# RWKV-6 attention and an MLP on one core: round 1's r-u-k sums from natural k and r, round 2's work one slot ahead, second products in runs of three

## The chip, the cores and the metric

One Trainium2 chip, one core. The metric is the device time in microseconds (us) of one execution, inputs and output in HBM. The kernel before takes 566.72 us (median of three runs, 566.61 to 567.1). The profiled execution has a span of 564.6 us.

## The reference, cut to what matters

B = 4 batches, H = 8 heads, S = 768 steps, D = 48; x has 384 columns, the MLP 1536 hidden ones. All is float32.

```python
# attention with decay, for every batch and head
for t in range(S):
    cur = einsum(u * k[t], v[t])                 # outer product
    y[t] = einsum(r[t], state + cur)             # the u term: (sum_d r*u*k) * v[t]
    state = w[t][:, None] * state + einsum(k[t], v[t])
x = y as (B, S, H*D)
# MLP
xn = (x - mean) / sqrt(var + 1e-6) * g_ln
out = x + maximum(xn @ w_ch1, 0) @ w_ch2
```

The change concerns the u term: for every step and head the sum over d of r\*u\*k, which multiplies v. It needs r and k as they lie in HBM ("natural": step in the partition), or turned (d in the partition), with a matmul to sum over partitions.

## The kernel before

A *unit* is four heads of one batch over 384 steps, a *round* two units (all eight heads), and there are eight rounds. A round goes through six levels: at each one, `quads` (TensorE, into `a_ps`) makes the products inside blocks of growing length, and `grow` (VectorE) multiplies r and k (`rkT`) by decays, so that the next level finds them ready. Then come `ends` (transposes of k, `kn_ps`), `states` (`kv`, then the chain `s` on VectorE) and `outputs` (`y`, then `x` on VectorE). Between these, `fill` places the steps of the MLP of the round before, three matmuls each, and a list of other tasks. TensorE, ScalarE (ACT), VectorE (DVE) and GpSimd (POOL) run their instructions in the order of this text; transfers given to `SP` may be issued earlier than they stand.

```python
def own_products(q, eng):                  # r*u*k in natural form
    rk = st[q]["ruk"] = p1.tile([P, TT, NH, D], F32, tag="rk")
    eng.tensor_tensor(out=rk, in0=nat["k"][q % 2][..., 0:D], in1=nat["r"][q % 2][..., 0:D], op=ALU.mult)
    eng.tensor_tensor(out=rk, in0=rk, in1=u_bc[...].broadcast_to(...), op=ALU.mult)
    if q >= FIRST * U:                     # FIRST = 3, U = 2
        k1 = nat["w"][0][..., 0:D]         # k of the step before
        eng.tensor_tensor(out=k1, in0=k1, in1=nat["r"][q % 2][..., 0:D], op=ALU.mult)

def own_sums(q):                           # VectorE: own, and next from round 3 on
    DVE.tensor_reduce(out=o, in_=st[q]["ruk"], axis=AX.X, op=ALU.add)
    ...

def products(q, eng=DVE):                  # rounds 0 and 1: r*k of the turned form
    eng.tensor_tensor(out=ruk, in0=a["r"], in1=a["k"], op=ALU.mult)

def product_sums(q):                       # 12 matmuls with u, 128x2 each: own_ps
    for pr in pairs:
        for c in range(TT):
            PE.matmul(ps[:, ts(pr * TT + c, 2)], a["ruk"][pr][:, ts(c, P)], sel[:, NP * g + pr], ...)
    ACT.copy(out=own, in_=ps)

def own_term(q, eng):                      # vo = v * own, and from round 3 on the step before's
    ...

def stage(q, nm, pr, eng=SP):              # 4 transfers into a "raw" buffer (4 of them): w_runs, k_runs, r_runs
def squares(q, nm, pr):                    # VectorE transposes from there into wT or rkT, rounds from 3 on

def mlp(rnd):
    for f in range(FC):                    # 12 steps of the first product: h_ps
        ...                                # three matmuls, then ACT relu: h
    groups = ((0, 1), (2,)) if rnd == 0 else ((0,), (1,), (2,))
    at = 0
    for group in groups:                   # second product: o_ps, one PSUM bank for each i
        for f in range(FC):
            converted(len(parts) - FC + f + 1)    # round 0: VectorE has joined so many weight parts
            for i in group:
                PE.matmul(ps[i], hs[f][:, ts(i, P)], w2_sb[:, f, :], start=f == 0, stop=f == FC - 1)
                at += 1
                if at % KC == 0 and f < FC - 1:
                    yield                  # KC = 3
        for i in group:
            DVE.tensor_tensor(out=o, in0=ps[i], in1=x[:, i], op=ALU.add)
            ...
```

h_ps and o_ps share two PSUM banks. In the MLP of round 0 the weights are still being split: ScalarE writes parts (`w_sb`, `held`, `rest`) and VectorE joins them. The loop of rounds, cut to what the change touches:

```python
for rnd in range(1, NR + 1):               # old, now, new: units of rnd-1, rnd, rnd+1
    for lev in range(NLEV):
        # states and outputs of old; quads, grow, keep of now
        ...
        if rnd == 2 and lev == 2:
            for q in now:
                take(DVE, q)               # own_products and own_sums, at once
                tasks += each(load, new[q % U :][:1], "kr")
        first = 3 if rnd == 2 else 1
        if rnd > 1 and new and first - 1 <= lev < first + 3:
            m = lev - first
            turns = [(new, "w"), (new[:1], "kr"), (new[1:], "kr")]
            if m >= 0:
                tasks += each(squares, *turns[m], pairs)
            if m < 2:
                tasks += each(stage, *turns[m + 1], pairs)
        ...
        fill(UNTIL[slot], tasks)           # MLP steps spread among the tasks
```

Of the kernel before, what the change touches and what calls it, by code (L numbers as in the profile page):

```python
# [9 lines left out]
F32 = mybir.dt.float32  # L10
# [42 lines left out]
def kernel(  # L53
# [68 lines left out]
    def load(q, which="wkr", eng=SP):  # L122
        for nm in which:
            for c in range(TT):
                eng.dma_start(
                    out=nat[nm][q % 2][:, c, :, 0:D],
                    in_=steps({"w": w, "k": k, "r": r}[nm], q, c),
                )
# [200 lines left out]
    def converted(n):  # L329
        while joined < n:  # L330
            join()
# [76 lines left out]

    def own_products(q, eng):
        b, f, g = units[q]  # L410
        rk = st[q]["ruk"] = p1.tile([P, TT, NH, D], F32, tag="rk", name=f"rk{q}")
        eng.tensor_tensor(
            out=rk, in0=nat["k"][q % 2][..., 0:D], in1=nat["r"][q % 2][..., 0:D], op=ALU.mult
        )
        eng.tensor_tensor(
            out=rk, in0=rk,
            in1=u_bc[:, ts(g, NH)][:, None].broadcast_to([P, TT, NH, D]), op=ALU.mult,
        )
        if q >= FIRST * U:
# [12 lines left out]
    def products(q, eng=DVE):  # L432
        a = st[q]

        if q < U:
            ruk = p2.tile([P, TT, H, D], F32, tag="x", name=f"ruk{q}")
            ruk = ruk.rearrange("p c h d -> p (c h d)")[:, 0:W]
        else:
            ruk = p2.tile([P, NK, P], F32, tag="kn", name=f"ruk{q}")
            ruk = ruk.rearrange("p k t -> p (k t)")  # L440
        a["ruk"] = [ruk[:, ts(pr, RN)] for pr in pairs]
        eng.tensor_tensor(out=ruk, in0=a["r"], in1=a["k"], op=ALU.mult)

# [265 lines left out]
    def mlp(rnd):  # L709
        b, f0 = rounds[rnd]  # L710
        x, xT, name = xs[b, f0], xTs[rnd], f"{b}_{f0}"
        hs = []
        for f in range(FC):
            converted(KC * (f * P // WC + 1))
            ps = ps_m.tile([P, RN], F32, tag="m", name=f"h_ps{name}_{f}")
            for kc in range(KC):
                PE.matmul(
                    ps, w1_sb[:, kc, ts(f, P)], xT[:, kc, :], start=kc == 0, stop=kc == KC - 1
                )
            hs.append(ph.tile([P, RN], F32, tag="h", name=f"h{name}_{f}"))  # L720
            ACT.activation(out=hs[f], in_=ps, func=AF.Relu)
            yield

        groups = ((0, 1), (2,)) if rnd == 0 else ((0,), (1,), (2,))
        at = 0
        for group in groups:
            ps = {
                i: ps_m.tile([P, H, D], F32, tag="m", name=f"o_ps{name}_{i}") for i in group
            }
            for f in range(FC):  # L730
                converted(len(parts) - FC + f + 1)
                for i in group:
                    PE.matmul(
                        ps[i].rearrange("p h d -> p (h d)"), hs[f][:, ts(i, P)],
                        w2_sb[:, f, :], start=f == 0, stop=f == FC - 1,
                    )
                    at += 1
                    if at % KC == 0 and f < FC - 1:
                        yield
            for i in group:  # L740
                o = p2.tile([P, H, D], F32, tag="o", name=f"o{name}_{i}")
                DVE.tensor_tensor(out=o, in0=ps[i], in1=x[:, i], op=ALU.add)
                SP.dma_start(
                    out=out[b, ds(f0 * RN + i * P, P), :].rearrange("t (h d) -> t h d", d=D),
                    in_=o,
                )
            yield
# [50 lines left out]
    FIRST = 3  # L798
    odd = const.tile([P, 1], F32, name="odd")

    def take(eng, q):

        own_products(q, eng)
        own_sums(q)


    (u0, u1), new = units_of(0), units_of(1)
    warm(8)
# [21 lines left out]
    begin()  # L830
    begin()
    load(new[1], "k", SPO)
    warm(3)
    grow(u1, 0)
    keep(0, 0)
# [22 lines left out]
    states(u0, "m")  # L858
    own_term(u0, POOL)
    finish(2)  # L860
    products(new[0], POOL)
    exchanged(u0)
    states(u1)
    product_sums(u1)
    own_term(u1, POOL)
    own_outputs(u0)
    warm(3, "t")
    outputs(u0)
# [14 lines left out]
    begin()  # L883
    join()
    join()
    products(new[1])
    run(each(turned_x, [0], range(KC)))
    mlps.append(mlp(0))

# [9 lines left out]
    for rnd in range(1, NR + 1):  # L899
# [3 lines left out]
        for lev in range(NLEV):  # L903
# [22 lines left out]
            if rnd == 1:  # L926
                if lev < 2:
                    tasks += each(load, new, "kr"[lev], [SPO])
                if lev == 2:
                    SPO.dma_start(  # L930
                        out=u_bc,
                        in_=bass.AP(
                            tensor=u.tensor, offset=u.offset, ap=[[0, P], [D, H], [1, D]]
                        ),
                    )
                    tasks += each(load_v, now, [SPO])
                if lev == 3:
                    tasks += each(load_vx, now, [SPO])
                if lev in (4, 5):
                    own_term(now[lev - 4], POOL)  # L940
# [5 lines left out]
                )  # L946
            if rnd == 2 and lev == 2:
                for q in now:
                    take(DVE, q)
                    tasks += each(load, new[q % U :][:1], "kr")  # L950
            if rnd == 2 and lev in (3, 4):
                tasks += each(own_term, now[lev - 3 :][:1], [POOL])
            if rnd > 2 and lev == 1:
                tasks += each(load, new, ["kr"])
            first = 3 if rnd == 2 else 1
            if rnd > 1 and new and first - 1 <= lev < first + 3:
                m = lev - first
                turns = [(new, "w"), (new[:1], "kr"), (new[1:], "kr")]
# [13 lines left out]
            if lev == 3 and rnd > 1:  # L972
                for q in now:
                    load_vx(q)
                for q in new:
                    load_v(q)
                if new:
                    load_before(new[0], k, 0)
                    load_before(new[0], v, 1)
                if rnd > 2:  # L980
                    moments(rnd - 1)
                    tasks = each(norm, [rnd - 1]) + tasks
            if lev == 4 and rnd > 2:
                tasks += each(turned_x, [rnd - 1], range(KC))
            if lev == 4 and rnd > 1:
                tasks += each(own_products, new[:1], [POOL])
            if lev == NLEV - 1:

                if now:
                    mlp_step()  # L990
                if rnd >= 2 and new:
                    own_sums(new[0])
                if rnd >= 2:
                    tasks += each(load_before, new[1:], [k], [0])
                    tasks += each(own_term, new[:1], [POOL])
                    tasks += each(load_before, new[1:], [v], [1])
                    tasks += each(own_products, new[1:], [POOL])
                    tasks += each(own_sums, new[1:]) + each(own_term, new[1:], [POOL])
                    if new:
                        tasks += each(totals, [rnd + 1], [POOL])  # L1000
                if now:
                    tasks = mixed(
                        tasks,
                        each(ends, now, pairs) + each(finish, [2, 2, 4])
                    )
                if rnd == 1:
                    tasks = [join] * JOINS[lev] + tasks + each(totals, [rnd + 1], [POOL])
            if rnd == 1 and lev < NLEV - 1:

                n = (1, 2, 2, 1, 0, 0)[lev] * NP  # L1010
                tasks += mixed(
                    [begin] * BEGINS[lev], [join] * JOINS[lev], ahead[:n],
                    each(product_sums, now) if lev == 1 else [],
                )
                del ahead[:n]
            fill(UNTIL[slot], tasks)
# [34 lines left out]
```

## Time and profile before

| | |
|---|---|
| time | 566.72 us |
| span of the profiled execution | 564.6 us |
| mean granted TensorE clock | 0.988 |
| DVE TENSOR_TENSOR ruk, 128x768 (3) | 951 ns each |
| POOL TENSOR_TENSOR ruk, 128x768 (1) | 1816 ns |
| POOL TENSOR_TENSOR rk, 128x576 | 1410 ns median |
| DVE TENSOR_TENSOR rk, 128x576 | 750 ns median of the first product |
| DVE TENSOR_REDUCE own, 128x576 to 128x12 | 752 ns median |
| ACT COPY own from own_ps | 170 ns |
| DVE STREAM_TRANSPOSE, four of w_runs | 2.9 us |

Durations are of single instructions, read from the groups of one tile. Engines: PE is TensorE, PEld its weight loads, DVE VectorE, ACT ScalarE, POOL GpSimd, SPq the sync engine's queue, which issues transfers. A float32 matmul of the source stands as two in the trace, so a step of three is x6. "A <- B" in a list of waits means that A waited for B. The names of lines (L49 and such) are those of a helper and tell little; tiles tell the operations apart.

### The profile page before, as it was taken

What the parts mean: (1) busy time and instruction counts of PE and PEld (TensorE: products, weight loads), DVE (VectorE), ACT (ScalarE), POOL (GpSimd) and SP (SyncE); (2) the same over time, 40 slices, a digit from 0 to 9 for tenths busy, and PEclk for the clock granted to TensorE, in tenths of its full rate; (3) what the DMA queues carried; (4) which work ended last, traced back from release to release, by engine and by line L of the source; (5) the groups of instructions that cost most, each with busy time, mean ns of one, the idle gap of its engine ahead of it and who ended that gap; (6) DMA issues with size and microseconds to landing.
All of it is one profiled execution on the core that took longest, in us unless ns stands there. A gap on an engine that the chain in (4) does not pass through costs nothing.

```text
span 564.6 us, 18202 instructions
## 1 busy us (share of the span) xinstructions
PE 548.6 (97%) x7898; PEld 359.3 (64%) x7898; DVE 332.1 (59%) x654; ACT 168.7 (30%) x363; POOL 134.8 (24%) x157
## 2 busy tenths in 40 slices
PE   9999998998889999999999999999999999999997
PEld 6777665675555666666666666666666666665554
DVE  4888998859777685757386655666472611130000
ACT  2576887502250015301421025201421025102200
POOL 6140010204194019401590029021640000000000
PEclk9899999999997999999999999999999999999999
DMA  9947887245566455646474646545200000000000
GB/s 231 195 127 144 209 215 193 57 94 100 127 153 145 123 125 119 137 102 147 95 140 99 139 106 136 119 120 118 58 1 2 31 15 1 2 29 15 0 15 28
DMA packets 141552, 56.64 MB, mean 100 GB/s; under 512 B 124448, under 2 KB 130720, under 8 KB 141472
## 3 DMA queue, kind: packets, MB, share of 16 engines
q1 hardware_dynamic: 139600, 54.88, 43.1%
q8 instruction: 62, 1.02, 0.8%
q10 hardware_dynamic: 1872, 0.59, 0.4%
q14 instruction: 18, 0.15, 0.1%
HBM read 48.66 MB, written 4.72 MB: 95 GB/s over the span
## 4 chain that ended last, share of the span: by engine, by line
PE 82%; DVE 9%; ACT 3%; DMA 2%; issue 2%; SPq 1%; POOL 0%; ACTq 0%; DVEq 0%; POOLq 0%
PE o_ps L49 33%; PE h_ps L49 27%; PE a_ps L49 9%; PE y L49 5%; DVE rkT L49 3%; DVE w_sb L49 2%; PE kv L49 2%; PE kn_ps L49 2%; DMA nat_r<-in_r_dram 1%; ACT rest L49 1%; PE xT_ps L49 1%; PE own_ps L49 1%; PE idle L49 1%; PE k_ps L49 1%; DVE A L49 1%
## 5 line engine op out<-in xcount | busy, mean ns | idle before, releaser
L49 PE MATMUL o_ps<-w_sb,h 128*128 128x384 f32 x576 | 200.2, 497 | 1.0 <-ACT h L49 1.0
L49 PE MATMUL h_ps<-xT,w_sb 128*128 128x384 f32 x576 | 196.4, 491 | 2.5 <-DVE o L49 1.4
L49 PEld LDWEIGHTS h_ps<-xT,w_sb 128*128 128x128 f32 x576 | 105.6, 190 | 70.3 <-DVE o L49 2.0
L49 PEld LDWEIGHTS o_ps<-w_sb,h 128*128 128x128 f32 x576 | 106.6, 192 | 67.8 <-issue 2.4
L49 DVE TENSOR_TENSOR rkT<-rkT,tot 128x768 f32<-128x768 f32 (+1 forms) x96 | 77.4, 849 | 27.6 <-issue 17.6
L49 ACT ACTIVATE h<-h_ps 128x384 f32<-128x384 f32 x96 | 46.9, 488 | 142.6 <-PE h_ps L49 142.4
L49 PEld LDWEIGHTS a_ps<-rkT 48*64 48x64 f32 x4128 | 65.7, 137 | 23.5 <-issue 12.5
L49 PE MATMUL a_ps<-rkT 48*64 48x32 f32 x4128 | 70.7, 221 | 3.4 <-DVE rkT L49 3.3
L49 DVE TENSOR_TENSOR o<-o_ps,x 128x384 f32<-128x384 f32 x24 | 13.3, 553 | 95.6 <-PE o_ps L49 95.5
L49 POOL TENSOR_TENSOR vo<-v,own 128x576 f32<-128x576 f32 x16 | 19.1, 1194 | 106.4 <-DVE own L49 62.5
L49 ACT ACTIVATE rstd<-mv,eps 128x3 f32<-128x3 f32 x8 | 2.4, 296 | 133.9 <-DVE mv L49 133.9
L49 DVE SCALAR_TENSOR_TENSOR s<-s,decay,kv 128x48 f32<-128x48 f32 x160 | 29.3, 256 | 18.9 <-PE kv L49 18.9
L49 POOL TENSOR_TENSOR nat_w<-nat_w,nat_r 128x576 f32<-128x576 f32 x10 | 14.4, 1436 | 103.1 <-DMA nat_w<-in_v_dram 70.5
L49 DVE COPY_PREDICATED A<-mask,a_ps 128x768 f32<-128x768 int8 x32 | 38.3, 1198 | 0.0
L49 DVE TENSOR_TENSOR x<-y,vo 128x288 f32<-128x288 f32 x32 | 13.1, 452 | 36.7 <-PE y L49 36.7
L49 ACT ACTIVATE xT<-xT_ps,g_sb 128x384 f32<-128x384 f32 x24 | 13.6, 579 | 48.4 <-PE xT_ps L49 48.4
L49 DVE TENSOR_TENSOR rkT<-rkT,wT 128x768 f32<-128x768 f32 x16 | 24.9, 1591 | 0.9 <-PE a_ps L49 0.8
L49 DVE TENSOR_REDUCE own<-rk 128x12 f32<-128x576 f32 x12 | 9.0, 749 | 23.6 <-POOL rk L49 23.5
L49 DVE TENSOR_SCALAR w_sb<-w_sb 128x384 f32<-128x384 f32 (+1 forms) x48 | 19.5, 407 | 0.8
L49 PEld LDWEIGHTS y<-v,A 64*64 64x64 f32 x384 | 13.4, 139 | 7.6 <-issue 4.4
L49 DVE STREAM_TRANSPOSE rkT<-r_runs 128x384 f32<-128x384 f32 x20 | 15.6, 840 | 3.2 <-DMA r_runs<-in_r_dram 3.2
L49 POOL TENSOR_TENSOR tot<-wT 128x768 f32<-128x768 f32 x6 | 12.4, 2072 | 20.2 <-DVE rkT L49 20.2
(88 smaller groups left out, 546.9 us busy)
## 6 DMA issues: line engine op xcount, KB each, us to landing
raw<-in_moe_w_ch_dram SPq DMA_DIRECT2D x24, 384.0 KB, 3.8
w_runs<-in_w_dram SPq DMA_DIRECT2D x79, 70.0 KB, 2.1
k_runs<-in_k_dram SPq DMA_DIRECT2D x79, 70.0 KB, 2.0
r_runs<-in_r_dram SPq DMA_DIRECT2D x79, 70.0 KB, 2.0
v<-in_v_dram SPq DMA_DIRECT2D x48, 96.0 KB, 2.9
out_dram<-o SPq DMA_DIRECT2D x24, 192.0 KB, 2.5
nat_r<-in_r_dram SPq DMA_DIRECT2D x42, 96.0 KB, 3.2
nat_k<-in_k_dram SPq DMA_DIRECT2D x42, 96.0 KB, 3.2
```

The source lines that it names most:

```text
L49: return lambda *args, **kw: self.tc.keep_in_program_order(f(*args, **kw))
```

## The change

It does four things.

- Round 1 takes its r-u-k sums from natural k and r, as later rounds do: two products on GpSimd for its first unit and on VectorE for its second, and reduces on VectorE, in place of a product of the turned form, 12 matmuls and a ScalarE copy for each unit. `u_bc`, which these products need, is loaded earlier.
- In the MLP of round 0 the second product goes in runs of three matmuls of one bank, in place of alternating between two.
- In round 2 the turning of round 3's w, k and r (stage and squares) is one slot, that is one level, earlier; the own products of round 2 become tasks.
- From round 2 on, GpSimd's chain (own products and own terms of the next round, with the transfers for it) is placed one slot earlier, and so are VectorE's sums of it.

The aim is to take work from TensorE and to have the next round's operands ready sooner.

```diff
     def own_products(q, eng):
-        rk = st[q]["ruk"] = p1.tile([P, TT, NH, D], F32, tag="rk", name=f"rk{q}")
+        if q < 2 * U:
+            rk = p2.tile([P, NK, P], F32, tag="kn", name=f"rk{q}")
+            ...
+        else:
+            rk = p1.tile([P, TT, NH, D], F32, tag="rk", name=f"rk{q}")
+        st.setdefault(q, {})["ruk"] = rk
...
-            for f in range(FC):
-                converted(len(parts) - FC + f + 1)
+            for f0_ in range(0, FC, KC):
+                converted(len(parts) - FC + f0_ + KC)
                 for i in group:
-                    PE.matmul(...hs[f]...)
-                    at += 1
-                    if at % KC == 0 and f < FC - 1:
+                    for f in range(f0_, f0_ + KC):
+                        PE.matmul(...hs[f]...)
+                    if f < FC - 1 or i != group[-1]:
                         yield
...
     load(new[1], "k", SPO)
+    SPO.dma_start(out=u_bc, ...)                 # was in round 1, level 2
...
-    products(new[0], POOL)
     exchanged(u0)
     states(u1)
     product_sums(u1)
     own_term(u1, POOL)
+    own_products(new[0], POOL)
...
-    products(new[1])
+    own_products(new[1], DVE)
...
             if rnd == 2 and lev == 2:
                 for q in now:
-                    take(DVE, q)
+                    tasks += each(own_products, [q], [DVE]) + each(own_sums, [q])
                     tasks += each(load, new[q % U :][:1], "kr")
+            if rnd >= 2 and lev == 2 and new:
+                tasks += each(load_before, new[:1], [k], [0]) + each(load_v, new[:1])
+                tasks += each(load_before, new[:1], [v], [1])
+            if rnd >= 2 and lev == 3:
+                tasks += each(load_v, new[1:])
...
-            first = 3 if rnd == 2 else 1
+            first = 2 if rnd == 2 else 1
...
             if lev == 3 and rnd > 1:
                 for q in now:
                     load_vx(q)
-                for q in new:
-                    load_v(q)
-                if new:
-                    load_before(new[0], k, 0)
-                    load_before(new[0], v, 1)
...
             if lev == 4 and rnd > 2:
                 tasks += each(turned_x, [rnd - 1], range(KC))
+                if rnd > 2 and new:
+                    tasks += each(own_sums, new[:1])
+            if lev == 3 and rnd > 1:
+                tasks += each(own_products, new[:1], [POOL])
             if lev == 4 and rnd > 1:
-                tasks += each(own_products, new[:1], [POOL])
+                if rnd == 2:
+                    tasks += each(own_sums, new[:1])
+                tasks += each(load_before, new[1:], [k], [0])
+                tasks += each(own_term, new[:1], [POOL])
+                tasks += each(load_before, new[1:], [v], [1])
+                tasks += each(own_products, new[1:], [POOL])
             if lev == NLEV - 1:
-                if rnd >= 2 and new:
-                    own_sums(new[0])
                 if rnd >= 2:
-                    tasks += each(load_before, new[1:], [k], [0])
-                    tasks += each(own_term, new[:1], [POOL])
-                    tasks += each(load_before, new[1:], [v], [1])
-                    tasks += each(own_products, new[1:], [POOL])
                     tasks += each(own_sums, new[1:]) + each(own_term, new[1:], [POOL])
...
-                    each(product_sums, now) if lev == 1 else [],
+                    each(own_sums, now) if lev == 1 else [],
```

More of the change, by code (lines that the diff above doesn't have):

```diff
@@ L410, in own_products @@
         b, f, g = units[q]
-        rk = st[q]["ruk"] = p1.tile([P, TT, NH, D], F32, tag="rk", name=f"rk{q}")
+        if q < 2 * U:
+            rk = p2.tile([P, NK, P], F32, tag="kn", name=f"rk{q}")
+            rk = rk.rearrange("p k t -> p (k t)")[:, 0 : TT * NH * D]
+            rk = rk.rearrange("p (c h d) -> p c h d", c=TT, h=NH)
+        else:
+            rk = p1.tile([P, TT, NH, D], F32, tag="rk", name=f"rk{q}")
+        st.setdefault(q, {})["ruk"] = rk
         eng.tensor_tensor(
@@ L433, in products @@
         a = st[q]
[L435 to L440, printed above, removed]
+        ruk = p2.tile([P, TT, H, D], F32, tag="x", name=f"ruk{q}")
+        ruk = ruk.rearrange("p c h d -> p (c h d)")[:, 0:W]
         a["ruk"] = [ruk[:, ts(pr, RN)] for pr in pairs]
@@ L724, in mlp @@
         groups = ((0, 1), (2,)) if rnd == 0 else ((0,), (1,), (2,))
-        at = 0
         for group in groups:
@@ L729, in mlp @@
             }
-            for f in range(FC):
-                converted(len(parts) - FC + f + 1)
+            for f0_ in range(0, FC, KC):
+                converted(len(parts) - FC + f0_ + KC)
                 for i in group:
[L733 to L736, printed above, removed]
-                    at += 1
-                    if at % KC == 0 and f < FC - 1:
+                    for f in range(f0_, f0_ + KC):
+                        PE.matmul(
+                            ps[i].rearrange("p h d -> p (h d)"), hs[f][:, ts(i, P)],
+                            w2_sb[:, f, :], start=f == 0, stop=f == FC - 1,
+                        )
+                    if f < FC - 1 or i != group[-1]:
                         yield
@@ L799 @@
     odd = const.tile([P, 1], F32, name="odd")
-    def take(eng, q):
-        own_products(q, eng)
-        own_sums(q)
     (u0, u1), new = units_of(0), units_of(1)
@@ L832 @@
     load(new[1], "k", SPO)
+    SPO.dma_start(
+        out=u_bc, in_=bass.AP(tensor=u.tensor, offset=u.offset, ap=[[0, P], [D, H], [1, D]])
+    )
     warm(3)
@@ L929 @@
                 if lev == 2:
[L930 to L935, printed above, removed]
                     tasks += each(load_v, now, [SPO])
```

## Prediction

> **What bounds the kernel now.** I read the page first: who is busy, and where the busy share dips.
>
> ```profile
> PE 548.6 (97%) x7898; PEld 359.3 (64%) x7898; DVE 332.1 (59%) x654; ACT 168.7 (30%) x363; POOL 134.8 (24%) x157
> ...
> PE   9999998998889999999999999999999999999997
> ...
> DVE  4888998859777685757386655666472611130000
> ...
> PEclk9899999999997999999999999999999999999999
> ```
>
> TensorE is busy for 97%; the dips are in slices 7 to 12, and the clock dips in slice 13. From 171 us on nothing is to be won: the windows show PE busy for all of 171.0-218.5, 218.5-281.1, 281.1-343.7 and 343.7-406.3. So the answer lies before 171 us. Next view, the windows of that part (columns: window, its length, then PE, PEld, DVE, ACT and POOL busy with counts, clock, DMA share, GB/s):
>
> ```profile
> 60.00:70.00 10.00, 9.37 (x51) 6.40 (x49) 9.35 (x19) 7.54 (x19) 0.00 (x0) 1.00 0.96 213
> ...
> 90.00:100.00 10.00, 8.95 (x121) 5.31 (x120) 8.92 (x21) 5.58 (x12) 0.42 (x1) 1.00 0.75 184
> ...
> 130.00:140.00 10.00, 8.63 (x118) 5.24 (x117) 9.83 (x10) 1.18 (x3) 5.43 (x4) 1.00 0.76 135
> 140.00:150.00 10.00, 10.00 (x214) 6.69 (x213) 8.03 (x11) 1.96 (x4) 2.85 (x2) 1.00 0.43 103
> 150.00:160.00 10.00, 8.50 (x79) 5.17 (x78) 7.69 (x12) 5.00 (x12) 4.58 (x4) 1.00 0.57 144
> 160.00:171.00 11.00, 8.16 (x126) 4.94 (x128) 8.60 (x19) 4.11 (x9) 10.21 (x8) 0.98 0.73 163
> ```
>
> Two stages have holes: 50-100 us, where VectorE is filled over 90% (it splits the MLP's weights there, beside round 1), and 120-171 us, round 2. PE's own waits in 118-172 us name the holes (who waits, for whom: us in total, times, longest), and short windows show what the last one does to the clock:
>
> ```profile
> PE a_ps L49 <- DVE rkT L49: 3.3, 3, 1.7
> PE h_ps L49 <- DVE o L49: 1.4, 1, 1.4
> PE kn_ps L49 <- DVE rkT L49: 1.2, 1, 1.2
> ```
>
> ```profile
> 168.00:170.00 2.00, 0.90 (x48) 0.82 (x48) 2.00 (x2) 0.00 (x0) 1.92 (x2) 1.00 0.70 167
> 170.00:171.00 1.00, 0.29 (x12) 0.29 (x15) 0.89 (x2) 0.00 (x0) 1.00 (x1) 0.73 0.63 129
> 171.00:172.00 1.00, 1.00 (x48) 1.00 (x43) 1.00 (x6) 0.00 (x0) 0.85 (x2) 0.50 0.50 89
> ```
>
> The holes at 167-171 us (1.68 + 1.15 us) are followed by half clock until about 177.9 us. That has a price of its own: 18 o_ps take 8.61 us there, 18 h_ps at full clock 6.07 us (at 142.15), and 48 a_ps 1.50 instead of 0.90 us; together about 3.1 us. Round 2 therefore holds 0.44 + 0.34 + 1.37 + 1.20 + 0.30 + 2.83 = 6.5 us of holes, plus 3.1 us of slow clock. Nearly 10 us is the most that the change can win there.
>
> What VectorE waits for in round 2 is seen in the sync engine's queue of transfers:
>
> ```profile
> 131.28 1.48 SPq L125 DMA_DIRECT2D nat_k<-in_k_dram  x3
> ...
> 141.84 3.59 SPq L163 DMA_DIRECT2D k_runs<-in_k_dram  x8
> 145.53 4.62 SPq L163 DMA_DIRECT2D r_runs<-in_r_dram  x8
> 150.24 3.61 SPq L163 DMA_DIRECT2D k_runs<-in_k_dram  x8
> 153.95 3.61 SPq L163 DMA_DIRECT2D r_runs<-in_r_dram  x8
> ```
>
> From 141.84 us it issues without a pause, 0.45 us each; VectorE's transposes wait 4.3 us in all for these.
>
> **What the Trainium skill says.** "SBUF — State Buffer", section "Who interferes with whom": a VectorE operation with two SBUF inputs and a GpSimd operation that reads SBUF exclude each other. The trace agrees: the two growing products of a level take 1.82 us at 143.73 us and 3.74 us at 136.42 us, where GpSimd works beside them. "PSUM — Partial Sum Buffer", section "Engine vs sequencer instructions": VectorE's queue is strictly first in, first out; so a squares transpose that waits for its transfer holds up all behind it. Here the transpose at 150.10 us sat 1.06 us behind its transfer, with the grows of level 5 behind it. "TensorE: Matmul & The Clock Gate", section "What's actually happening": a window of about 3.4 us with little work halves the clock. The 0.50 after 170.7 us, behind 3.7 us with 0.9 us of work, agrees.
>
> **The change, part by part.**
>
> *Round 1's sums.* Removed: 24 own_ps matmuls in two runs, at 62.9 and 66.8 us, 1.24 us each on PE's path, 2.5 us; one VectorE product of 0.95 us, one GpSimd product of 1.82 us, two ScalarE copies of 0.17 us. Added: on GpSimd two products of 1.41 us (the rk row), 2.8 us, at about 40-43 us, where it is idle afterwards; on VectorE two products of 0.75 us and two reduces of 0.75 us, 3.0 us. Net on VectorE +2.05 us, in a stage where it is full from 46 to 104 us. It had one wait of 0.43 us there, for a_ps at 71.4 us, which PE's lead absorbs, so some +1.6 us remain. That passes on: VectorE frees the buffer for ScalarE's "rest" at 79.84 us, and ScalarE then runs unbroken to 92.46 us. PE's saved 2.5 us are lost in waits for that chain, which becomes 1.6 us later.
>
> *Runs of three.* Now the second o_ps matmul needs the second PSUM bank, which the last h eviction frees: PE sat 0.98 us until 92.50. In the new order three matmuls (1.94 us) go to the first bank before. With the chain 1.6 us later: last h_ps begins at 90.0 (88.34 + 1.6), ends 92.2; three o_ps until 94.1; the bank is free at 94.1; three more until 96.1. Before, these two steps ended at 95.96. Sum of the two parts: +0.2 us. The u_bc transfer (one issue of 0.42 us, landing after 4.0 us) moves to about 28 us, in front of waits for weights: 0.
>
> *Round 2's turning one slot ahead.* VectorE gets the four transposes of w (2.8 us) in level 2, ahead of the last o of the first MLP. Own products and sums stand before that as they did, until 135.95. So o ends at 135.95 + 2.8 + 0.55 = 139.3 us instead of 136.5, and PE's second h_ps, which needs its bank, waits 4.1 instead of 1.37 us. The transfers: reloading k and r still begins at 131.28, behind the own products, and takes until 137.7; then 32 runs at 0.45 us, 14.5 us, and one out: 152.6 us instead of 157.66. They land 1.9 us later, 154.5. In the new order level 4 holds the second unit's turning (0.85 us behind the last landing) and the first unit's sums (2.07 us), before level 5's grows: 157.5 us instead of 152.5. The kn transposes therefore start at about 158.0 instead of 153.09.
>
> From there things turn. PE has 13.9 us of work to the end of kv (153.09 to 167.0 before): 172 us. VectorE has behind level 5 only the second unit's sums, which end at about 165.6 by GpSimd's chain (own term 3.7, products 2.8, k product 1.4 us), states 2.0, and the grow 3.7: 171.3 us. So PE finds round 3's grows ready: no hole there and no fall of the clock. Its quads end at 173.5 instead of 172.2 (+1.3), but the 18 o_ps take 6.0 instead of 8.6 us: −2.6. Round 2: −1.3 us, if the new holes (4 us at 135, up to 3.5 us at 154) do not slow the clock themselves. The first of them may well do, since it is as long as the one that did. Then PE comes late to the kn transposes, which wait until 158 anyway, and little is added. A fall after the second costs about +3.1: round 2 at +1.8.
>
> *GpSimd's chain in rounds 3 to 7.* Removed: VectorE's wait for POOL's rk (23.5 us in all, 5.6 the longest). PE doesn't wait for VectorE there, so 0; added are sums of 2.07 us before level 5's grow, which had about 2 us to spare (208.74 to the kn transposes at 211.28): 0 to +0.3 a round.
>
> Sum: +0.2 and −1.3 (two thirds) or +1.8 (one third), +0.3: about 566.7. I go below it to **565.8 us**, because the order of the transfers is the weakest step, and it errs against the change: each transfer that gets out earlier than I place it shortens both holes.
>
> **Rivals.** *The full gain:* all holes of round 2 and its slow clock go, 557 to 560 us. For it: VectorE's waits there are waits for transfers (4.3 us) and GpSimd (2.2 us), and the change attacks both. Against: level 5 now stands behind more VectorE work and the same queue. *A new wait takes the place of the old:* o and kn hold PE back and the clock falls in both places, 569 to 571 us. For it: first-in-first-out order and the sums above. *VectorE's extra 2 us in round 1 reach the end undamped:* 568 us; for it its 93% share in 60-70 us; against, the bank wait that goes. *Hidden anyway:* all parts are swallowed, 566-567 us.
>
> **Range and chances.** The low end lies somewhat over half way from the sum to the full gain, the high end in the middle of the second rival: 561.0 to 570.0 us. A gain over 2% needs 555.4 us, more than all holes of round 2 with the clock; a loss over 2% needs 578 us, three falls of the clock. So 0.02, 0.96 and 0.02.
>
> **What would show it.** No own_ps at 63-68 us, and the first o_ps after the change in an unbroken run of six (parts 1 and 2). PE h_ps waiting for o near 135 us for 4 us rather than 1.4, and kn_ps at 158 us behind rkT (part 3). PEclk 1.00 in 171-178 us, with 18 o_ps in 6.0 us: this carries the gain. PE full in all rounds from 171 us on. The prediction is wrong if the clock falls after 158 us, if k_runs start well before 137 us, or if rounds 3 to 7 show new waits of PE.

## The result and the profile after

| | before | after |
|---|---|---|
| time, median, us | 566.91 (566.61 to 567.87) | 573.14 (571.53 to 575.31) |
| ratio, with 95% interval | | 1.0109 [1.0071, 1.0148] |
| span of the profiled execution, us | 564.6 | 570.7 |

The change costs 1.1%. The prediction of 565.8 us was too low, and 573.14 lies above its range. The page of the kernel after shows first where TensorE and its clock dip:

```profile
PE 544.3 (95%) x7874; PEld 354.6 (62%) x7874; DVE 342.9 (60%) x657; ACT 168.5 (30%) x361; POOL 135.2 (24%) x158
...
PE   8999979998789999999999999999999999999997
...
PEclk9999989999979999999999999999999999999999
```

A slice is 14.27 us. Slice 6 (71 to 86 us) holds a wait of h_ps for ScalarE's h in round 1, of 2.7 us. The deepest dip behind it is slice 11, 143 to 157 us (8 before, now 7), and the clock dips right behind, in slice 12 instead of 13. The windows of round 2 say the same in microseconds (window, length, then PE, PEld, DVE, ACT, POOL busy, clock, DMA share, GB/s):

```profile
130.00:140.00 10.00, 8.10 (x116) 4.69 (x115) 9.83 (x12) 0.98 (x2) 5.03 (x4) 1.00 0.83 142
140.00:150.00 10.00, 9.11 (x157) 5.67 (x159) 8.08 (x9) 1.96 (x4) 3.42 (x2) 1.00 0.58 149
150.00:160.00 10.00, 3.52 (x76) 2.27 (x70) 6.93 (x11) 0.49 (x1) 1.76 (x2) 0.87 0.49 119
160.00:170.00 10.00, 10.00 (x78) 6.41 (x77) 7.91 (x16) 6.05 (x14) 9.65 (x8) 0.78 0.59 130
```

TensorE works 3.52 of the 10 us from 150 to 160 (8.50 before), then ten full microseconds at a clock of 0.78. Its list of waits in 117 to 182 us (total, times, longest) has one large entry:

```profile
PE kn_ps L49 <- DVE rkT L49: 6.5, 1, 6.5
PE h_ps L49 <- DVE o L49: 1.3, 1, 1.3
PE a_ps L49 <- DVE rkT L49: 1.3, 2, 0.9
```

Milestones of the two traces, set side by side, place the loss:

| stretch | before, us | after, us | difference |
|---|---|---|---|
| start to kn_ps of round 1 | 99.5 | 98.8 | -0.7 |
| from there to kn_ps of round 2 | 53.6 | 61.0 | +7.4 |
| from there to the y that opens round 3 | 27.6 | 23.0 | -4.6 |
| from there to the first kv of round 3 | 37.8 | 40.2 | +2.4 |
| kv of round 3 to kv of round 6, three rounds | 3 x 62.6 | 3 x 63.1 | +1.5 |

Their sum, 6.0 us, is close to the difference of the spans, 6.1 us. So there are three losses: 2.8 us in round 2 (7.4 less 4.6), 2.4 us in round 3 and half a microsecond in each of rounds 4 to 6. The first row is not a gain to be trusted: eight profiles of kernels that are the same up to there (the kernel after and its variants below) reach one and the same transpose (r_ps) between 43.6 and 46.7 us, the later ones with a clock below 1.00 before it.

What VectorE did before the late kn_ps is in its timeline (start, duration; in brackets the idle time before and who ended it):

```profile
153.01 0.85 DVE L49 STREAM_TRANSPOSE rkT<-k_runs 128x384 f32<-128x384 f32 x1 [1.14 <-DMA k_runs<-in_k_dram]
...
156.60 0.85 DVE L49 STREAM_TRANSPOSE rkT<-r_runs 128x384 f32<-128x384 f32 x1 [0.81 <-DMA r_runs<-in_r_dram]
157.30 0.69 DVE L49 TENSOR_REDUCE own<-rk 128x12 f32<-128x576 f32 x1
157.91 0.74 DVE L49 TENSOR_REDUCE next<-nat_w 128x12 f32<-128x576 f32 x1
158.68 0.57 DVE L49 TENSOR_SCALAR next<-next,odd 128x12 f32<-128x12 f32 x1
159.17 5.33 DVE L49 TENSOR_TENSOR rkT<-rkT,tot 128x384 f32<-128x384 f32 x4
```

The turning of k and r ends at 157.4 us, each transpose waiting for its transfer; then come the sums, and only then level 5's four grows, the first of which kn_ps needs. The grows take 5.33 us, with GpSimd's own term beside them, against 1.92 us before:

```profile
152.50 1.92 DVE L49 TENSOR_TENSOR rkT<-rkT,tot 128x384 f32<-128x384 f32 x4
```

Where the transfers come from is in the sync engine's queue:

```profile
130.55 1.48 SPq L125 DMA_DIRECT2D nat_k<-in_k_dram  x3
...
137.41 3.69 SPq L163 DMA_DIRECT2D k_runs<-in_k_dram  x8
141.20 4.82 SPq L163 DMA_DIRECT2D r_runs<-in_r_dram  x8
...
146.58 3.64 SPq L163 DMA_DIRECT2D k_runs<-in_k_dram  x8
150.32 4.66 SPq L163 DMA_DIRECT2D r_runs<-in_r_dram  x8
```

The reload of natural k and r begins at 130.55 us, when round 2's own products have released them, and the runs stand behind it in the same queue. Moving the turning one level ahead put all eight transposes ahead of level 5's grows in VectorE's queue; before, four of them stood behind, and the grows began at 152.50 us. The transfers' begin moved by 4.4 us and their end by 2.6 (the last is issued by 154.98 us, 157.56 before), less than the 7.5 us of a level (before, the a_ps of two levels start at 140.62 and 148.16 us).

Round 3 has a smaller copy of this. VectorE's grows of its level 5, before and after, and then PE's timeline after:

```profile
208.74 2.14 DVE L49 TENSOR_TENSOR rkT<-rkT,tot 128x384 f32<-128x384 f32 x4 [0.36 <-PE a_ps L49]
```

```profile
213.33 6.29 DVE L49 TENSOR_TENSOR rkT<-rkT,tot 128x384 f32<-128x384 f32 x4
```

```profile
214.65 0.87 PE L49 MATMUL kn_ps<-ident,rkT 128*128 128x128 f32 x6 [0.48 <-DVE rkT L49]
216.42 0.52 PE L49 MATMUL kn_ps<-ident,rkT 128*128 128x128 f32 x3 [0.90 <-DVE rkT L49]
```

kn_ps did not wait there before. Two things stand ahead of it that did not: GpSimd works beside the grows, and the runs for the turning are later (the last is issued by 205.96 us, 197.07 before), with transfers for GpSimd's chain (nat_w and v) now ahead of them in the queue.

### The profile page after: what moved, and what is told of

Its sections match the earlier page's. It is cut to its first block, busy times and chain, and to the rows that moved or that the text cites. A ratio compares the mean times of both kernels' runs of the same rounds, so it can differ in the third digit from the quotient of the medians.

```text
span 570.7 us, 18138 instructions
## 1 busy us (share of the span) xinstructions
PE 544.3 (95%) x7874; PEld 354.6 (62%) x7874; DVE 342.9 (60%) x657; ACT 168.5 (30%) x361; POOL 135.2 (24%) x158
## 4 chain that ended last, share of the span: by engine, by line
PE 79%; DVE 11%; SPq 3%; issue 2%; DMA 2%; ACT 2%; POOL 1%; DVEq 0%; ACTq 0%; POOLq 0%
PE o_ps L49 31%; PE h_ps L49 28%; PE a_ps L49 8%; PE y L49 4%; DVE rkT L49 3%; DVE w_sb L49 3%; SPq L163 2%; PE kv L49 2%; PE kn_ps L49 2%; DVE A L49 1%; DMA r_runs<-in_r_dram 1%; PE xT_ps L49 1%; PE r_ps L49 1%; DVE stats L49 1%; PE k_ps L49 1%
## 5 line engine op out<-in xcount | busy, mean ns | idle before, releaser
L49 PE MATMUL h_ps<-xT,w_sb 128*128 128x384 f32 x576 | 199.3, 496 | 5.8 <-ACT h L49 3.3
L49 PE MATMUL o_ps<-w_sb,h 128*128 128x384 f32 x576 | 196.6, 491 | 0.0
L49 PEld LDWEIGHTS h_ps<-xT,w_sb 128*128 128x128 f32 x576 | 106.8, 192 | 74.9 <-ACT h L49 4.8
L49 DVE TENSOR_TENSOR rkT<-rkT,tot 128x768 f32<-128x768 f32 (+1 forms) x96 | 93.6, 1017 | 25.1 <-issue 16.3
L49 DVE TENSOR_TENSOR o<-o_ps,x 128x384 f32<-128x384 f32 x24 | 13.3, 552 | 89.0 <-PE o_ps L49 89.0
L49 ACT ACTIVATE xT<-xT_ps,g_sb 128x384 f32<-128x384 f32 x24 | 13.3, 579 | 41.6 <-PE xT_ps L49 41.6
L49 PE MATMUL kn_ps<-ident,rkT 128*128 128x128 f32 x96 | 15.7, 293 | 9.7 <-DVE rkT L49 7.9
L49 PEld LDWEIGHTS kn_ps<-ident,rkT 128*128 128x128 f32 x96 | 11.7, 148 | 16.6 <-DVE rkT L49 8.2
L49 ACT COPY kn<-kn_ps 128x384 f32<-128x384 f32 x32 | 14.4, 479 | 15.5 <-PE kn_ps L49 15.4
L49 POOL TENSOR_TENSOR nat_w<-nat_w,nat_r 128x576 f32<-128x576 f32 x10 | 16.5, 1653 | 6.6 <-DMA nat_w<-in_k_dram 6.6
L49 POOL TENSOR_TENSOR rk<-nat_k,nat_r 128x576 f32<-128x576 f32 x11 | 16.8, 1531 | 4.9 <-DMA nat_r<-in_r_dram 4.7
```

The lines of the kernel that those rows point to most:

```text
L49: return lambda *args, **kw: self.tc.keep_in_program_order(f(*args, **kw))
```

## The experiments

Three theories stood behind them. **A**: the sums and GpSimd's chain, now ahead of and beside level 5's grows, hold kn_ps back. **B**: the turning does, with the transfers behind it. **C**: the extra 2 us of VectorE in round 1 reach the end. Rounds 3 to 7 were open. All ratios are to the kernel before, on the same chip.

### One part at a time

*Part 1, round 1's sums, alone:*

```diff
-    products(new[0], POOL)
+    own_products(new[0], POOL)
-    products(new[1])
+    own_products(new[1], DVE)
-    each(product_sums, now) if lev == 1 else [],
+    each(own_sums, now) if lev == 1 else [],
```

> The kernel before with round 1's sums alone (and u_bc loaded early). If round 2 and GpSimd's chain carry the loss (theories A and B), this costs within 1 us of before, 566 to 568 us: TensorE loses 2.5 us of own_ps and waits instead for the VectorE chain, which is 1.6 us longer. If round 1's extra VectorE work carries it (theory C), it is 569 us or more.

Measured: 566.55 us, 1.0004 [0.9982, 1.0027]. In round 1 h_ps waits for ScalarE's h (2.8 us the longest), so PE's saved 2.5 us end in that wait, as the prediction had it; nothing is left at the end. Theory C falls.

*Part 2, runs of three, alone:*

```diff
-            for f in range(FC):
+            for f0_ in range(0, FC, KC):
                 for i in group:
-                    PE.matmul(...hs[f]...)
+                    for f in range(f0_, f0_ + KC):
+                        PE.matmul(...hs[f]...)
```

> The kernel before with the second products of the first MLP in runs of three alone. The 0.98 us wait ahead of the second o_ps goes; what is behind it in round 2 is bound by VectorE and the transfers, so 0 to 1 us faster by all theories. A larger change would mean that the order in which PSUM banks are given out matters, as the changed kernel shows a third h_ps, not the second, waiting for o.

Measured: 564.58 us, 0.9978 [0.9962, 0.9993]: the wait of 0.98 us for the second bank is gone, and it shows in the time. Both parts together:

> The kernel before with round 1's sums and the runs of three, without the other two parts. If the loss lies in round 2's turning and in GpSimd's chain, this is no slower than before, 564.5 to 567 us, since the runs of three take away the wait that the longer VectorE chain would fill. If the parts need each other, it is slower than before by over 1 us.

Measured: 566.84 us, 1.001 [0.999, 1.0029]. Part 2's gain does not show when part 1 holds ScalarE's chain back (h_ps waits up to 2.6 us for h, 0.5 us in part 2 alone); the difference of the ratios is not clear of the noise.

*Part 3, the turning, alone:*

```diff
-                    take(DVE, q)
+                    tasks += each(own_products, [q], [DVE]) + each(own_sums, [q])
-            first = 3 if rnd == 2 else 1
+            first = 2 if rnd == 2 else 1
```

> The kernel before with round 2's turning one level earlier and own products as tasks alone. Theory B (the turning itself: transposes that wait for transfers stand ahead of level 5's grow): 3 us or more slower, kn_ps behind rkT at about 156 us and the clock halved after it. Theory A (GpSimd's own term beside level 5's grow): within 1.5 us of before, since the sums still stand behind the grow.

Measured: 567.9 us, 1.0033 [1.0016, 1.0051]; PE's timeline shows the hole before kn_ps appear, though GpSimd's chain is where it was:

```profile
157.17 2.41 PE L49 MATMUL kn_ps<-ident,rkT 128*128 128x128 f32 x9 [2.86 <-DVE rkT L49]
```

*Part 4, GpSimd's chain, alone* (own products of the next round in level 3's list, sums and own term in level 4's, in place of one level later each):

> The kernel before with GpSimd's chain and its sums one level earlier alone. Theory A: level 5's grow takes over 5 us for its four products in rounds 2 to 6 instead of 1.9, kn_ps waits in rounds 2 and 3, and 3 to 5 us are lost in all, of which 0.5 us a round from round 3 on by the run of nine kn_ps. Theory B: within 1 us of before in round 2, at most 2.5 us lost in later rounds.

Measured: 568.01 us, 1.0024 [1.0007, 1.0042]. Level 5's grows take 5.33 us in round 2 and 6.30 in round 3, kn_ps of round 2 waits 2.5 us, and the rounds from 3 on last 63.1 instead of 62.6 us. The excesses of the three measurements (0.10 + 0.33 + 0.24%) make 0.67%; the whole change costs 1.09%, more than the sum, but with intervals of about 0.2 to 0.4% on each figure this is not clear of the noise.

The trace of part 4 shows where its loss lies. From kn_ps of round 1 to the y that opens round 3 it takes 77.7 us, 3.5 us less than before (81.2); round 3, from that y to the next round's, takes 60.6 instead of 56.8 us. With the turning alone these are 83.0 and 56.8 us. So the turning costs in round 2, while GpSimd's chain wins there and loses in round 3 and later.

### Undoing one part of the change

*Sums and own term back behind the grows:*

```diff
-                if rnd > 2 and new:
-                    tasks += each(own_sums, new[:1])
...
-                tasks += each(own_term, new[:1], [POOL])          # level 4
...
+                if rnd >= 2 and new:                              # level 5, behind its grow
+                    own_sums(new[0])
+                    tasks += each(own_term, new[:1], [POOL])
```

> The changed kernel with the sums of the next round's first unit, its own term and the second unit's products put back behind level 5's grow; the turning stays early. Theory A (sums ahead of the grow, and GpSimd's own term beside it): the grow's four products are back at about 2 us, kn_ps starts 4 to 5 us earlier in round 2, does not wait in round 3, and the time is 566 to 568 us. Theory B (early turning): the kn_ps wait in round 2 stays at 3 us or more and the time above 569 us.

Measured: 571.68 us, 1.0088 [1.0056, 1.012]. VectorE's timeline shows that the grows are as short as before, PE's timeline that kn_ps waits all the same:

```profile
158.35 1.92 DVE L49 TENSOR_TENSOR rkT<-rkT,tot 128x384 f32<-128x384 f32 x4
```

```profile
158.94 2.43 PE L49 MATMUL kn_ps<-ident,rkT 128*128 128x128 f32 x9 [5.33 <-DVE rkT L49]
```

Theory A is refuted as the main cause of round 2's hole: without the sums and without GpSimd beside the grows they still begin at 158.35 us, because VectorE waits for the transfers. The Trainium skill, "SBUF — State Buffer", section "Who interferes with whom", says that a VectorE operation with two SBUF inputs and a GpSimd operation that reads SBUF exclude each other; the trace agrees (5.33 against 1.92 us for the same four products). Here most of it lay beside a wait that was there anyway: the two ratios, 1.0088 and 1.0109, lie within each other's intervals. Round 3 still takes 59.3 us, 2.5 more than before: there a_ps waits 2.33 us for VectorE behind the late transfers. So it stays open how much of round 3's loss is GpSimd's disturbance and how much the transfers.

*The turning put back to level 3:*

```diff
-            first = 2 if rnd == 2 else 1
+            first = 3 if rnd == 2 else 1
```

> The changed kernel with round 2's turning put back one level. Theory B: kn_ps starts 3 us or more earlier in round 2, and 3 us or more of the time come back. Theory A: the grow of level 5 still takes over 4 us and kn_ps waits 2 us or more; at most 2.5 us come back.

Measured: 568.67 us, 1.0042 [1.0024, 1.006]. PE's timeline:

```profile
151.89 0.88 PE L49 MATMUL kn_ps<-ident,rkT 128*128 128x128 f32 x6 [0.99 <-DVE rkT L49]
```

One number brings 0.67% back (1.0109 to 1.0042) and kn_ps 7.9 us forward, with the grows still at 5.33 and 6.29 us. Theory B carries the larger loss; the half microsecond in each later round is still there. By this trace (of a run 2.7 us under the median) round 2 is 4.6 us shorter than before and round 3 3.7 us longer: without the early turning GpSimd's chain wins in round 2, as it does alone, and the turning spoils that.

*Four empty tasks,* to give level 5's list of the later rounds its former length (seven; in the kernel after three):

```diff
+                        tasks = [lambda: None] * 4 + tasks
```

> The changed kernel with four empty tasks in the list of level 5, so that kn_ps transposes and MLP steps alternate as in the kernel before (two in a run, not three). No engine gets more or less work. If the loss of 0.5 us in each round from 3 on is the order of these, kn_ps x9 becomes x6 and x3 again and 2 to 2.5 us come back; if it is GpSimd's contention, nothing changes.

Measured: 571.03 us, 1.0081 [1.0051, 1.0111]; the rounds last 62.6 us again. The gain of 1.6 us is less than expected, and by the ratios alone not clear of the noise; the periods in the traces show it. Why is seen in PE's timeline of round 5, in the kernel after:

```profile
342.56 0.55 PE L49 MATMUL kn_ps<-ident,rkT 128*128 128x128 f32 x3 [0.30 <-ACT kn L49]
342.95 2.10 PE L49 MATMUL h_ps<-xT,w_sb 128*128 128x384 f32 x6
```

and with the four empty tasks:

```profile
342.19 0.82 PE L49 MATMUL kn_ps<-ident,rkT 128*128 128x128 f32 x6
342.85 2.10 PE L49 MATMUL h_ps<-xT,w_sb 128*128 128x384 f32 x6
344.78 0.82 PE L49 MATMUL kn_ps<-ident,rkT 128*128 128x128 f32 x6
```

`fill` spreads MLP steps among a list by its length. With three tasks it leaves a third transpose directly behind two others, and that one waits 0.30 us until ScalarE has emptied a PSUM bank; with seven, an MLP step lies between. The period goes with this order in every kernel run: 63.1 us with the short list, 62.6 with the long one, with GpSimd beside the grows (this run) as without (sums and own term put back). The 0.30 us wait is seen; the other 0.2 us are not split further.

*Both repairs together:*

> The changed kernel with round 2's turning put back and the four empty tasks in level 5: what is left of the change is round 1's sums, the runs of three and GpSimd's chain. If the two repairs add up (3.8 and 2.1 us to the kernels measured so far), 566 to 567.5 us, the same as before. If they overlap: 568 us or more.

Measured: 566.87 us, 1.0004 [0.9984, 1.0024]: the level of parts 1 and 2 alone (1.001). The two causes account for the loss. The rest of part 4 (GpSimd's chain one slot earlier) is then worth nothing in the time, but as a sum of two effects: in this run's trace round 2 is 3.4 us shorter than before (77.7 us to the y that opens round 3), and round 3 1.9 us longer.

### What makes the turning late, and what the clock adds

*Half as many transfers for round 3's k and r,* twice the rows in each and the same bytes. They take the rows in another order, so what round 3 computes isn't the reference's:

```diff
+            if nm != "w" and q // U == 3:
+                eng.dma_start(out=t[ds(HP * j, HP), 0:ROW],
+                    in_=bass.AP(tensor=src.tensor, offset=first, ap=[[NS * D // 2, HP], [1, ROW]]))
+                continue
```

> The changed kernel, but in round 2 the k and r of round 3 are staged with 16 transfers instead of 32, the same bytes in rows of another order; so what round 3 computes is not the reference's, its work and sizes are. Theory B (level 5's grow stands behind the issue of 32 transfers): VectorE's waits for k_runs and r_runs (4.9 us in round 2) go mostly, kn_ps of round 2 starts 3 to 5 us earlier after that of round 1 (61.0 us in the changed kernel), and the time is 569 to 571 us. If VectorE's own work ahead of the grow is what counts: less than 1.5 us earlier, 572 to 573 us.

Measured: 567.46 us, 1.0021 [1.0003, 1.004], better than expected. The sync engine's queue, and then PE's timeline:

```profile
137.33 2.54 SPq L158 DMA_DIRECT2D k_runs<-in_k_dram  x4
...
146.50 2.46 SPq L158 DMA_DIRECT2D r_runs<-in_r_dram  x4
```

```profile
154.46 0.88 PE L49 MATMUL kn_ps<-ident,rkT 128*128 128x128 f32 x6 [1.50 <-DVE rkT L49]
```

The transfers start where they did in the kernel after and are all issued by 148.96 instead of 154.98 us. kn_ps comes 5.3 us earlier, the clock does not fall, and some 5 us of the change's 6 are gone. The number of issues, not the bytes, makes the turning late. The Trainium skill, "DMA: Bandwidth & Descriptors", section "Rules for kernel authors", advises to join many small transfers and names 64 KB as the size below which they are mostly overhead. These have 70.0 KB each by the profile page, and joining still paid: two issues took 1.23 us (2.46 / 2) where four took 1.8 (3.64 / 2).

*The clock kept up in the hole* by seven idle matmuls that nothing waits for:

```diff
+                if rnd == 2:
+                    warm(21)          # 7 matmuls, behind level 5's last MLP step, ahead of kn_ps
```

> The changed kernel with seven idle matmuls (5.9 us of TensorE) put into the hole before round 2's kn_ps. The hole stays as long, as VectorE sets its end. If the fall of the clock behind it has a price of its own: kn_ps x9 takes 1.5 instead of 2.4 us and the h_ps x6 behind it 2.1 instead of 3.2, and 1.5 to 2 us come back, 571 to 571.5 us. If the fall is hidden by what VectorE does next: no change.

Measured: 574.29 us, 1.0121 [1.0082, 1.016]: no gain. PE's timeline (the first line is the idle work):

```profile
156.00 4.90 PE L49 MATMUL idle<-nought 128*128 128x384 f32 x14
162.34 0.87 PE L49 MATMUL kn_ps<-ident,rkT 128*128 128x128 f32 x6 [1.44 <-DVE rkT L49]
...
164.21 2.10 PE L49 MATMUL h_ps<-xT,w_sb 128*128 128x384 f32 x6
```

The next h_ps take 2.10 us where they took 3.25, and from kn_ps to the second kv it is 13.3 instead of 14.8 us. But from there to round 3's first kv it is 49.9 instead of 48.4: those 1.5 us lie beside work that ends later anyway. kn_ps of round 3 starts 54.9 us behind that of round 2 in both kernels, and waits 1.41 and 0.90 us for its grows where it waited 0.48 and 0.90. So the fall of the clock, which the prediction priced at 3.1 us, is not a separate loss here; the hole is.

*The own products of round 2 two levels ahead,* in the kernel after, so that the reload and the transfers behind it can begin earlier:

```diff
-            if rnd == 2 and lev == 2:
                 for q in now:                                     # now in level 0
-                    tasks += each(own_products, [q], [DVE]) + each(own_sums, [q])
+                    own_products(q, DVE)
+                    own_sums(q)
                     tasks += each(load, new[q % U :][:1], "kr")
```

> The changed kernel with round 2's own products, sums and the reloads of k and r at level 0 of round 2 instead of level 2. If the late start of the transfers is the cause of its loss in round 2: the kn_ps of round 2 no longer wait more than 1.5 us and the time falls to 564 to 567 us (2 us of the loss stay, by the order of kn_ps in rounds 3 to 6). If the early turning or GpSimd's chain carry it: 570 us or more.

Measured: 567.2 us, 1.0008 [0.9986, 1.0029], slightly above what was expected, and so is the wait of kn_ps (2.10 us, at most 1.5 were expected). The first reload goes out at 112.03 us instead of 130.55, and the runs start at 133.22 instead of 137.41; PE's timeline:

```profile
155.77 0.87 PE L49 MATMUL kn_ps<-ident,rkT 128*128 128x128 f32 x6 [2.10 <-DVE rkT L49]
```

Some 5.7 us of the loss are gone. The edit moves VectorE's own products out of level 2 too, so the transfers' begin is not alone in it; the run with half the transfers leaves VectorE's work in its place. By its trace round 2 is 1.9 us shorter than before, round 3 1.1 us and rounds 4 to 6 1.5 us longer. The clock falls here too (0.50 in 158 to 160 us).

### A version that beats both

The same move in the kernel before, with runs of three and without parts 1, 3 and 4:

```diff
+            # in the branch for round 2, level 0
+                for q in now:
+                    take(DVE, q)
+                    tasks += each(load, new[q % U :][:1], "kr")
```

> A new version: the kernel before with the runs of three, and round 2's own products and sums, with the reloading of k and r behind them, moved from level 2 to level 0 of that round, where VectorE idles 3.6 us for y. Turning and GpSimd's chain stay as before. If round 2 is bound by the chain that begins at these products (VectorE 5.3 us, then 12 transfers, then 32), o comes 5 us earlier, the holes of 1.4, 1.2 and 2.8 us shrink and the clock does not fall at 171 us: 558 to 562 us. If something else in round 2 holds it, as level 5's transposes behind level 3's: within 1.5 us of the 564.6 us that the runs of three had alone.

Measured: 560.81 us, 0.9909 [0.9876, 0.9941], clear of the 0.9978 [0.9962, 0.9993] that the runs of three had alone. Windows of the same stretch in three kernels, before, after and this one (columns as above):

```profile
120.00:171.00 51.00, 44.51 (x748) 28.78 (x750) 42.68 (x66) 13.98 (x30) 23.07 (x16) 0.99 0.57 125
```

```profile
120.00:171.00 51.00, 40.93 (x597) 25.86 (x590) 43.01 (x64) 12.34 (x26) 20.87 (x15) 0.93 0.55 118
```

```profile
120.00:171.00 51.00, 46.78 (x756) 30.34 (x749) 40.24 (x73) 14.85 (x32) 20.33 (x18) 1.00 0.61 135
```

PE's idle time falls from 6.5 (before) and 10.1 (after) to 4.2 us, at full clock. And with the turning one level ahead on top (`first = 2`):

> The version with the runs of three and round 2's own products at level 0, with round 2's turning one level earlier as in the change; from that version this differs in the turning alone. If the early turning did harm only through transfers that start late: within 1 us of that version, 560 to 562 us, or faster. If it does harm by itself (more VectorE work ahead of o and of level 5's grow): 563 us or more.

Measured: 564.47 us, 0.9954 [0.9928, 0.9979], the harmful side of what was expected. kn_ps is on time at 153.06 us, but VectorE waits 4.2 us for the runs of r and 5.7 us for GpSimd's rk, and a_ps waits 3.2 us. The gap to the version without it is 0.45%, and the two intervals just overlap, so only the direction is supported: the turning's place buys nothing once its transfers start early.

## Why the prediction was wrong

- **Parts 1 and 2: right.** +0.2 us was predicted, +0.1% measured with an interval that holds zero (1.001). No own_ps stands at 63 to 68 us, the six o_ps run unbroken, and the 2.5 us saved became the wait of h_ps for ScalarE's h.
- **The failed step, first half: rounds 3 to 7.** The sum puts +0.3 us for all of them (its own line, 0 to 0.3 a round, would allow 1.5). Measured from the y that opens round 3 to the end are +4.0: 2.4 in round 3 and 0.5 in each of rounds 4 to 6. The term looked at VectorE's sums of 2.07 us, with about 2 us to spare. It left out GpSimd's own term beside the grows (6.29 instead of 2.14 us) and the transfers ahead of the runs, behind which kn_ps of round 3 waits 1.4 us, and in rounds 4 to 6 the order of the transposes in a shorter list, which is no engine's extra work. The runs put this down to part 4: round 3 takes 56.8 us with the turning alone, as before, and 60.6 us with GpSimd's chain alone. (That undoing the turning brings more back is no contradiction: it lets GpSimd's chain win in round 2, which the sum for round 2 takes together with the turning.)
- **The failed step, second half: the transfers' term of round 2.** The prediction put 32 runs at 0.45 us, 14.5 us, ending at 152.6 us. They took from 137.41 to 154.98, 17.6 us: two of the four sets of eight needed 4.8 and 4.7 us instead of 3.6, each by one issue of 1.62 and 1.47 us, and an output transfer stands between. The kernel before has such a set too (r_runs at 145.53 us, 4.62 us, in the prediction's own fence), and its working passed over it. So the last transpose ended at 157.4 us, where the prediction had the sums and all end at 157.5. kn_ps started at 159.77 instead of about 158.0.
- **The hole ahead of o: wrong size.** 4.1 us was predicted for h_ps's wait for o, 1.32 us came (and 0.58 us of waiting for ScalarE's h), since it was the third h_ps after that point, not the second, that needed o's bank. PE therefore lost little there and came to kn_ps with more time to wait: the two holes foreseen (4 and up to 3.5 us) became mainly one, of 6.48 us.
- **Level 5's grows: one thing left out.** The prediction took them at their time without GpSimd, whose own term the change moves beside them: 5.33 instead of 1.92 us. Where that was undone and nothing else, the time stayed within its interval, so this is no large part of round 2's loss.
- **The clock: the less likely branch came.** It was given a third of the chance and +1.8 us. It fell around 158 us (0.87 in 156 to 158 us, 0.50 behind), which the text had named as a sign of its being wrong. The Trainium skill, "TensorE: Matmul & The Clock Gate", section "What's actually happening", puts it down to a window of some 3.4 us with little work; the kernel after agrees, with a hole of 6.48 us and this window at its end:

```profile
158.00:160.00 2.00, 0.23 (x1) 0.23 (x2) 1.97 (x4) 0.00 (x0) 1.76 (x2) 0.50 0.32 79
```

- **What followed in round 2 was right.** In 171 to 178 us the clock is 1.00, the 18 o_ps take 6.1 us, and round 3's first grows are ready: 4.6 of the 7.4 us are regained there. The fall itself cost less than the 3.1 us of the prediction: from kn_ps to the second kv it is 14.8 us, 13.0 before. So its branch with the fall, +1.8 us for round 2, comes near the 2.8 measured, partly by luck: kn_ps was placed 1.8 us too early, and the fall was priced 1.3 us too high. But "PE full in all rounds from 171 us on" did not come, and new waits in these rounds were another sign that it named: from 178 to 218 us it is busy for 38.22 of 40 us.
- **Small slips.** The terms of the sum give 567.0 and not 566.7 us, and the two growing products at 143.73 us take 1.78 us, not 1.82. With the fall certain they give 569.0 us; with 4.0 in place of 0.3 us for rounds 3 to 7 as well, 572.7 us, near the 573.14 measured. So the odds of the clock alone don't explain the miss; the rounds from 3 on do.
- **The rivals.** "A new wait takes the place of the old" is what happened, at 573.1 instead of 569 to 571 us; the fall of the clock that it rested on was not what cost (the run with idle matmuls). "Hidden anyway" holds for the time of GpSimd's chain alone, once the list has its old length, by a gain in round 2 and a loss in round 3.

## What to carry to other kernels

When an engine waits for a chain of transfers, follow the chain back to what lets its first link be issued and move that into an idle slot; moving the consumer ahead in a first-in-first-out queue only makes it wait with more work behind it. Check also that the next stage can take a gain: 1.5 us that the idle matmuls won in round 2 ended in waits of round 3. Time such a chain from first issue to last as a whole, from the trace, not as a count times the median issue. And when tasks move between lists that another routine interleaves with filler, look at the order that comes out on every engine: a list that becomes shorter can put three users of two banks in a row.

## What was not expected of the hardware

- The number of issues bounded the staging: four transfers of 70.0 KB took 1.8 us of the sync engine's queue, two of twice the size 1.23 us, and the halved queue was worth 0.9% of the kernel's time.
- An issue on the sync engine's queue takes 0.42 us at the median, but three that were read singly took 1.42, 1.47 and 1.62 us (one in the kernel before, two after), and in each of these moments, and not between them, the trace has one transfer of the queue that it calls "instruction". Whether the one causes the other, no run tested.
- Four VectorE products take 5.33 us in round 2 and 6.29 us in round 3 beside GpSimd, 1.92 and 2.14 us before: 2.8 and 2.9 times as long.
- Half a clock for 7 us behind the hole was worth 1.5 us locally and nothing at the end.
